# Attention into two expert stages: PSUM banks handed out a second time, sums of squares on other engines, copies queued behind the sigmoids

## The chip, the cores and the metric

One core of one Trainium2 chip. The metric is device microseconds of one launch. TensorE (PE) does the matrix products, with a queue of its own for weight loads (PEld); ScalarE (ACT), VectorE (DVE) and GpSimd (POOL) do the rest; SyncE's queue (SP) issues nearly all transfers. Each engine takes its instructions in the order in which the program gives them out. PSUM, in which products are accumulated, has eight banks of 512 f32 per partition.

## The reference

```python
# q, k, v: 4 x 12 heads x 448 x 64, f32
attn = 1 / (1 + exp(-(q @ k.T / 8 - log(448))))          # a sigmoid, no softmax
x = (attn @ v), heads side by side                       # 1792 x 768
xn = x / sqrt(mean(x * x) + 1e-6) * rms_g
g = xn @ w_gate;  val = xn @ w_val                       # 768 -> 1536
x = (g * sigmoid(g) * val) @ w_out                       # 1536 -> 768
logits = x @ gate                                        # 8 experts
out = top probability * (relu(x @ w1[e]) @ w2[e])        # the token's expert e
```

## The kernel before, in words

The order of all instructions is written out by hand; a helper adds the semaphores, from which instructions touch which tile.

**Attention** (L498, driven by the loop at L1054) takes 84 steps t, 21 (`QS`) for each of four batches. A step puts eight score products on PE (`quarters`, L528) into a PSUM tile of two banks, `two[t % 2]`; ACT takes the sigmoid (`weights`, L534) into SBUF; two steps later PE multiplies by v (`weighted`, L545) into two of the banks `one`. Seven steps do two pairs of heads. When a pair is done, `both` (L567) has ACT copy one bank (L575) and, a step later, DVE add the other (L576): that is x. `squares` (L579) then has POOL square x (L585, L582 for a batch's first pair) and add it to the batch's sum (L586). In step t, `step()` gives out what has come due, ahead of `weights(t)`; `then(1, ...)` called just before `step()` comes due in that same call.

`normalise` (L614) runs beside the next batch's steps: PE sums over partitions (L618), four small DVE operations, twelve on POOL (L633 to L636), ACT spreads the result (L640), PE turns it (L644), ACT copies it (L646), and DVE scales x in six steps (L650); batch 0 is also split in two for the exact products (ACT L670, DVE L675), the others go to DRAM. The last batch's `normalise` is a part of the attention generator and runs beside the first expert stage.

Beside attention, 64-bit weights are loaded and narrowed to 32 bits by three DVE operations each (`narrow`, L213, L217, L221; 36 pieces, 108 operations): one per call of `next(conv)` at L1068, the rest within the first batch of the first expert stage, where `operations_due` (L52) says how many. From the 13th piece on, the result goes to DRAM out of two buffers `wn` (L228).

**First expert stage** (`moe1`, L279, for each of four batches): 12 units of gate and value products, then 6 of the output product. A unit is four pieces of nine 128x128x448 products (`three`, L270, lines L273 to L275). A unit of the first kind has two banks, `pg` and `pv`, of `mm_bank`, three banks given out in turn. Two pieces after `pg` is started ACT takes its sigmoid (L281), DVE multiplies by `pg` (L282); after the next unit's first piece DVE multiplies by `pv` (L287), ACT and DVE split the result (L288, L289). An output unit has one bank; ACT copies it (L314), DVE subtracts and transposes it (L317, L320). Weights are split for the next unit by ACT (L243) and DVE (L246).

**Second expert stage** (L1184): four batches of 14 blocks, eight on w1 into `mm` banks (evicted by ACT L760 and DVE L761) and six on w2 into `sc` banks (DVE L781, L782); routing and the tokens of other experts run between blocks (L900, L924).

The banks of these two stages are slices of attention's tiles (L152 to L157):

```python
two = [ps.tile([128, 2, 512], F32, tag="two", name=f"two{i}", bufs=2) for i in range(2)]
one = [ps.tile([128, 512], F32, tag="one", name=f"one{i}", bufs=4) for i in range(4)]
fixed["mm"] = [two[0][:, 0, :], two[0][:, 1, :], two[1][:, 0, :]]
fixed["sc"] = [two[1][:, 1, :], one[3]]
fixed["av"] = [one[0], one[1]]
fixed["mi"] = [one[2]]
```

So two `mm` banks belong to the tile `two0`, and the third shares `two1` with an `sc` bank. `logit_bank` (L308) is the `mi` bank, and in the last batch one taken out of `mm`.

Of the kernel before, what the change touches and what calls it, by code (L numbers as in the profile page):

```python
# [9 lines left out]
F32 = mybir.dt.float32  # L10
# [38 lines left out]
LAG = 2  # L49


def operations_due(n):  # L52

    return int(n < 60 and n % 3 < 2)


CONST = {}
# [36 lines left out]
def block_kernel(ctx, tc, qkp, v, wg, wv, wo, g, gate, w1, w2, consts, out):  # L94
# [3 lines left out]
    def opened(name, side="left", **kw):  # L98
        s = ExitStack()
        return s, s.enter_context(tc.tile_pool(name=name, bufs=1, side=side, **kw))  # L100

    s_c, cpool = opened("cpool")
    s_d, dram = opened("dram", space=DRAM)
    s_p, ps = opened("ps", space=PSUM)
    s_k, keep = opened("keep")
    s_w, wp = opened("wp", reuse_waits="tile")
    s_x, xp = opened("xp", reuse_waits="tile")
# [43 lines left out]

    two = [ps.tile([128, 2, 512], F32, tag="two", name=f"two{i}", bufs=2) for i in range(2)]  # L152
    one = [ps.tile([128, 512], F32, tag="one", name=f"one{i}", bufs=4) for i in range(4)]
    fixed["mm"] = [two[0][:, 0, :], two[0][:, 1, :], two[1][:, 0, :]]
    fixed["sc"] = [two[1][:, 1, :], one[3]]
    fixed["av"] = [one[0], one[1]]
    fixed["mi"] = [one[2]]  # L157

    clock = [0]
    due = {}  # L160
# [337 lines left out]
    def attention():  # L498

        sums, score, weight = {}, {}, {}  # L500
        halves = [slice(0, D), slice(D, 2 * D)]
        last = NC - 1
        order = []
        for u in range(0, B * H // 2, 2):
            order += [(u, c) for c in range(NC)] + [(u + 1, c) for c in range(last)]
        due_at = {}
        now = [0]
        av = [one[0][:, :S], one[1][:, :S]]
        odd = [one[2][:, :S], one[3][:, :S]]

        def then(steps, f, *a):
            due_at.setdefault(now[0] + steps, []).append((f, a))

        def step():
            now[0] += 1
            for f, a in due_at.pop(now[0], []):
                f(*a)

        def quarters(t):
            u, c = order[t]  # L520
            for x, h in enumerate(halves):
                for i, o in enumerate(halves):
                    if c < last:
                        r, head, k = raw_a[u], h, S + 128 * c + D * i
                    else:

                        r, head, k = raw_a[u + x], halves[x ^ i], S + 128 * c
                    nc.tensor.matmul(  # L528
                        two[t % 2][o, x, :S], r[head, k : k + D], r[head, :S], start=True, stop=True
                    )  # L530

        def weights(t):
            a = aq.tile([128, 2, S], F32, tag="a", name="a", bufs=3)
            nc.scalar.activation(  # L534
                out=a, in_=two[t % 2][:, :, :S], func=AF.Sigmoid, bias=logs, scale=1.0 / math.sqrt(D)
            )
            weight[t] = a

        def add_up(u, c, x, i, a):

            v4 = raw_v[u].rearrange("s (c j d) -> s c j d", j=2, d=D)
            y = u % 2
            k = x ^ i ^ y
            first, end = (0, last if k == 0 else last - 1) if y == 0 else (last if k == 0 else 0, last - 1)
            nc.tensor.matmul(  # L545
                sums[u][k][halves[x]], v4[halves[i], c, x, :], a[halves[i]], start=(c == first), stop=(c == end)
            )

        def weighted(t):
            u, c = order[t]  # L550
            a = weight.pop(t)
            if c == 0 and u % 2 == 0:
                sums[u] = av
            elif c == 0:
                sums[u] = odd
            if c == last:
                sums[u + 1] = odd
            for x in range(2):
                for i in range(2):
                    if c < last:  # L560
                        add_up(u, c, x, i, a[:, x, :])
                    else:
                        add_up(u + x, c, x ^ i, i, a[:, x, :])
            if c == last - u % 2:
                then(1, both, u)

        def both(u):  # L567
            b, p = divmod(u, H // 2)
            if p == 0:
                pool, tag = (aq, "xt") if b % 2 else (keep, "x2_")  # L570
                xts[b] = [pool.tile([128, S], F32, tag=f"{tag}{k}", name="xt") for k in range(KD)]
                sss[b] = aq.tile([128, S], F32, tag="ss", name="ss", bufs=2)
            x = xts[b][p]
            p0, p1 = (sums[u][1], sums[u][0]) if u % 2 else (sums[u][0], sums[u][1])
            nc.scalar.copy(out=x, in_=p0)  # L575
            then(1, lambda: nc.vector.tensor_tensor(out=x, in0=p1, in1=x, op=ALU.add))  # L576
            then(2, squares, b, p)

        def squares(b, p):  # L579
            x = xts[b][p]  # L580
            if p == 0:
                nc.gpsimd.tensor_tensor(out=sss[b], in0=x, in1=x, op=ALU.mult)  # L582
            else:
                sq = aq.tile([128, S], F32, tag="sq", name="sq")
                nc.gpsimd.tensor_tensor(out=sq, in0=x, in1=x, op=ALU.mult)  # L585
                nc.gpsimd.tensor_tensor(out=sss[b], in0=sss[b], in1=sq, op=ALU.add)  # L586

        load_pair(0)
        load_v(0)
        load_pair(1)  # L590
        normal = iter(())
        for t in range(B * QS + LAG):
            if t < B * QS:
                u, c = order[t]
                if c == 0:
                    load_v(u + 1)
                    load_pair(u + 2)
                quarters(t)
            if t >= LAG:
                weighted(t - LAG)  # L600
            step()
            if t < B * QS:
                weights(t)
            if t >= QS and t % QS == 5:
                normal = normalise(t // QS - 1, odd[1])
            next(normal, None)
            yield
        while due_at:
            step()
            yield  # L610
        yield
        yield from normalise(B - 1, one[3])

    def normalise(b, bank):  # L614
        xt, ss = xts[b], sss[b]
# [16 lines left out]
        for _ in range(3):  # L632
            nc.gpsimd.tensor_tensor(out=ta, in0=ya, in1=ya, op=ALU.mult)  # L633
            nc.gpsimd.tensor_tensor(out=ta, in0=ta, in1=va, op=ALU.mult)
            nc.gpsimd.tensor_scalar(out=ta, in0=ta, scalar1=1.5, scalar2=None, op0=ALU.add)
            nc.gpsimd.tensor_tensor(out=ya, in0=ya, in1=ta, op=ALU.mult)  # L636
        yield
        yield
        yb = aq.tile([CT, NC, 128], F32, tag="yb", name="yb")
# [410 lines left out]
        yield  # L1050


    att = attention()
    for n in range(B * QS + LAG):  # L1054
        next(att)
        if n < RAW:
            load_64(n)
        if n == 10:
            nc.sync.dma_start(out=cst, in_=consts)
            nc.sync.dma_start(out=g_sb, in_=g)  # L1060
            nc.sync.dma_start(out=gate_sb, in_=gate)
        if n == 15:
            nc.scalar.copy(out=gate_2[:, :, :E], in_=gate_sb)
            nc.vector.tensor_tensor(
                out=gate_2[:, :, E:], in0=gate_sb, in1=f32(gate_2[:, :, :E]), op=ALU.subtract
            )
        if 2 <= n < 40 or n % 4 < 3:
            next(conv)  # L1068
        tick()
        if n in (60, 62):  # L1070
            split_w(0, n // 2 - 30)
    for b in range(B):
        routing = route(b - 1) if b > 0 else iter(())
        coming = iter(())
        for n, _ in enumerate(moe1(b)):
            next(att, None)
            if n == 4 * KF and b + 1 < B:
                coming = bring_x(b + 1)
            next(coming, None)
            tick()  # L1080
            if b == 0:
                if to_store:
                    c, w = to_store.pop(0)
                    nc.sync.dma_start(out=w32d[c // 2][c % 2], in_=w)
                for _ in range(operations_due(n)):
                    next(conv, None)
            elif n >= 2 and n % 2 == 0:
                next(routing, None)
            if b == 3:
                if n == 0:  # L1090
                    s_a.close()
                    s_r.close()
                    open_raw()
                    load_x(0)
                    e0 = own_expert(0)
                if n >= 2 and n % 2 == 0 and n < 2 * KD + 2:
                    load_row(w1, ph2["w1r"], e0, n // 2 - 1)
                if n == 49:
                    s_x.close()
                    ph2["s1"], ph2["ring1"] = opened("ring1", side="right", reuse_waits="tile")  # L1100
                if n in (62, 66):
                    split_block((n - 62) // 4)
        if b + 1 == B:
            settle()
# [160 lines left out]
```

## Time and profile before

| | us |
|---|---|
| median of three runs | 1023.4 (1023.02 to 1023.63) |
| the profiled execution, its own time | 1022.94 |
| its span, first to last instruction | 1021.2 |

The profile shows one execution. Its span is 1.74 us shorter than that execution's time. PE is busy for 93% of the span, DVE 53%, ACT 35%, POOL 9%; a busy PE is modelled with overlapping products, so intervals from start to start say more than durations. "Idle before" names what ended an engine's wait.

### The profile page before, as it was taken

The page shows a single profiled execution, that of the slowest core. Times are in us where ns is not written, and L with a number is a line of the kernel's source. Part 1 is how long each engine was busy: PE and PEld are TensorE (multiplying, and loading weights), DVE is VectorE, ACT ScalarE, POOL GpSimd, SP SyncE. Part 2 cuts the span into 40 slices and gives each one's busy share as a digit, 9 for nine tenths or more (in the row PEclk, how much of TensorE's full clock was granted, in tenths as well). Part 3 has the DMA queues.
Part 4 walks back from the last instruction along what each step waited for, and adds up shares of the span by engine and source line. Part 5 has one row for each costly group of instructions (what it writes and reads, how often), then busy time and mean ns, then how long its engine had stood idle before and what let it go on. Part 6 is the DMA issues. An engine that isn't in the chain of part 4 may idle for free.

```text
span 1021.2 us, 14782 instructions
## 1 busy us (share of the span) xinstructions
PE 953.7 (93%) x5646; PEld 782.7 (77%) x5646; DVE 546.2 (53%) x890; ACT 352.3 (35%) x508; POOL 87.5 (9%) x103
## 2 busy tenths in 40 slices
PE   8989998999999999999998999999988999989997
PEld 3434347888878888888887888889878878878887
DVE  5886777776435544435644436444355634334345
ACT  5676762323323333323333323332222132222130
POOL 1555553000000000000000000000000000000000
PEclk9999999999999999999999999999999999999999
DMA  8959988765753324562434694335376749829633
GB/s 322 335 198 350 327 315 281 272 235 184 222 167 94 109 93 147 171 180 75 124 102 148 173 317 175 122 93 143 113 210 241 202 146 334 283 69 318 167 55 57
DMA packets 128509, 195.72 MB, mean 192 GB/s; under 512 B 63321, under 2 KB 85209, under 8 KB 128432
## 3 DMA queue, kind: packets, MB, share of 16 engines
q1 hardware_dynamic: 120832, 192.58, 57.7%
q10 hardware_dynamic: 7456, 1.61, 0.8%
q8 instruction: 45, 0.74, 0.3%
q0 software_dynamic: 144, 0.53, 0.3%
q14 instruction: 32, 0.26, 0.1%
HBM read 152.54 MB, written 42.00 MB: 191 GB/s over the span
## 4 chain that ended last, share of the span: by engine, by line
PE 83%; DVE 7%; ACT 3%; DMA 2%; issue 2%; POOL 1%; SPq 1%; ACTq 0%; DVEq 0%; POOLq 0%
PE two L273 23%; PE two L275 21%; PE two L274 21%; PE two L528 4%; PE one L545 4%; PE one L273 2%; PE one L275 2%; PE one L274 2%; DVE sg L287 1%; ACT sg L281 1%; PE two L900 1%; DVE hl L761 1%; ACT a L534 1%; DMA w<-in_wg 1%; DMA w32d<-w32h 1%
## 5 line engine op out<-in xcount | busy, mean ns | idle before, releaser
L273 PE MATMUL two<-xh,wh 128*128 128x448 f32 x576 | 214.8, 373 | 21.0 <-DVE sg L287 13.0
L275 PE MATMUL two<-xh,wl 128*128 128x448 f32 x576 | 210.7, 366 | 0.0
L274 PE MATMUL two<-xl,wh 128*128 128x448 f32 x576 | 210.6, 366 | 0.0
L246 DVE TENSOR_TENSOR wl<-w,wh 128x768 fp32r<-128x768 f32 x132 | 124.8, 949 | 33.6 <-ACT wh L243 29.2
L273 PEld LDWEIGHTS two<-xh,wh 128*128 128x128 f32 x576 | 108.2, 188 | 41.9 <-DVE sg L287 18.5
L243 ACT CAST wh<-w 128x768 fp32r<-128x768 f32 x132 | 109.7, 831 | 47.2 <-PE two L274 33.0
L273 PE MATMUL two<-hs,wh 128*128 128x448 f32 x288 | 106.7, 371 | 11.7 <-DVE xr L320 8.0
L275 PEld LDWEIGHTS two<-xh,wl 128*128 128x128 f32 x576 | 108.2, 188 | 9.1
L274 PEld LDWEIGHTS two<-xl,wh 128*128 128x128 f32 x576 | 108.3, 188 | 8.3
L275 PE MATMUL two<-hs,wl 128*128 128x448 f32 x288 | 105.3, 366 | 0.0
L274 PE MATMUL two<-hs,wh 128*128 128x448 f32 x288 | 105.3, 366 | 0.0
L288 ACT CAST hs<-sg 128x448 fp32r<-128x448 f32 x48 | 27.2, 568 | 183.4 <-DVE sg L287 183.4
L534 ACT ACTIVATE a<-two,logs 128x896 f32<-128x896 f32 x84 | 83.1, 1010 | 19.1 <-PE two L528 19.1
L528 PE MATMUL two<-rqk 64*64 64x448 f32 x672 | 82.9, 552 | 6.1 <-DMA rqk<-in_qkp 3.8
L273 PE MATMUL two<-xd,w1h 128*128 128x448 f32 x192 | 72.2, 376 | 12.0 <-DVE hl L761 12.0
L545 PE MATMUL one<-a,rv 64*64 64x448 f32 x672 | 81.5, 537 | 0.9 <-DMA rv<-in_v 0.9
L282 DVE TENSOR_TENSOR sg<-two,sg 128x448 f32<-128x448 f32 x48 | 29.8, 622 | 83.8 <-PE two L275 76.1
L273 PEld LDWEIGHTS two<-hs,wh 128*128 128x128 f32 x288 | 54.1, 188 | 22.0 <-DVE xr L320 10.3
L274 PE MATMUL two<-xd,w1h 128*128 128x448 f32 x192 | 70.8, 369 | 0.0
L275 PE MATMUL two<-xd,w1l 128*128 128x448 f32 x192 | 70.8, 369 | 0.0
L317 DVE TENSOR_TENSOR x2s<-two,x2s 128x448 fp32r<-128x448 f32 x24 | 15.0, 625 | 85.7 <-ACT x2s L314 47.9
L528 PEld LDWEIGHTS two<-rqk 64*64 64x64 f32 x672 | 25.4, 134 | 46.1 <-issue 22.6
(185 smaller groups left out, 1303.0 us busy)
## 6 DMA issues: line engine op xcount, KB each, us to landing
w<-w32d SPq DMA_DIRECT2D x132, 384.0 KB, 3.6
w1r<-in_w SPq DMA_DIRECT2D x24, 512.0 KB, 6.3
w2r<-in_w SPq DMA_DIRECT2D x32, 384.0 KB, 6.7
x2s<-x2s SPq DMA_DIRECT2D x48, 224.0 KB, 2.0
xd<-x2s SPq DMA_DIRECT2D x8, 1344.0 KB, 9.7
rqk<-in_qkp SPq DMA_DIRECT2D x23, 448.0 KB, 6.4
w<-in_wg SPq DMA_DIRECT2D x12, 768.0 KB, 6.6
w<-in_wv SPq DMA_DIRECT2D x12, 768.0 KB, 6.4
```

The source lines that it names most:

```text
L243: nc.scalar.copy(out=h, in_=w3)
L246: nc.vector.tensor_tensor(out=l, in0=w3, in1=f32(h), op=ALU.subtract)
L273: nc.tensor.matmul(p, wh, xh, start=(n == 0), stop=False)
L274: nc.tensor.matmul(p, wh, xl, start=False, stop=False)
L275: nc.tensor.matmul(p, wl, xh, start=False, stop=last)
L281: nc.scalar.activation(out=t, in_=p, func=AF.Sigmoid)
L282: later(1, lambda: nc.vector.tensor_tensor(out=t, in0=p, in1=t, op=ALU.mult))
L288: nc.scalar.copy(out=hs[:, 0, :], in_=t)
L317: nc.vector.tensor_tensor(out=l, in0=p, in1=f32(h), op=ALU.subtract)
L528: nc.tensor.matmul(two[t % 2][o, x, :S], r[head, k : k + D], r[head, :S], start=True, stop=True)
L534: nc.scalar.activation(out=a, in_=two[t % 2][:, :, :S], func=AF.Sigmoid, bias=logs, scale=1.0 / math.sqrt(D))
L545: nc.tensor.matmul(sums[u][k][halves[x]], v4[halves[i], c, x, :], a[halves[i]], start=(c == first), stop=(c == end))
```

## The change

PSUM is closed after attention and opened again as eight tiles of one bank each: three `mm`, two `sc`, two `av`, one `mi`. Squares move from POOL to ACT, and their sums to DVE a step later. `step()` comes after `weights(t)`, so what is due in a step is queued behind that step's sigmoid. `normalise` waits one more step ahead of L640. The conversions have another pattern: from step 2 on one in each step, none in steps 11 to 17 of each 21 from the second batch's on, and in the first expert stage three for each four pieces (48 places) where there were two for each three (40). The attention loop now runs until attention has nothing due, and the last `normalise` starts from the loop over `moe1`, in a new `sc` bank.

```diff
 def operations_due(n):
-    return int(n < 60 and n % 3 < 2)
+    return int(n < 64 and n % 4 < 3)
...
-    s_p, ps = opened("ps", space=PSUM)
+    s_p, ps = opened("ps", space=PSUM, reuse_waits="tile")
...
-    fixed["mm"] = [two[0][:, 0, :], two[0][:, 1, :], two[1][:, 0, :]]
-    fixed["sc"] = [two[1][:, 1, :], one[3]]
-    fixed["av"] = [one[0], one[1]]
-    fixed["mi"] = [one[2]]
...
             if p == 0:
-                nc.gpsimd.tensor_tensor(out=sss[b], in0=x, in1=x, op=ALU.mult)
+                nc.scalar.square(out=sss[b], in_=x)
             else:
                 sq = aq.tile([128, S], F32, tag="sq", name="sq")
-                nc.gpsimd.tensor_tensor(out=sq, in0=x, in1=x, op=ALU.mult)
-                nc.gpsimd.tensor_tensor(out=sss[b], in0=sss[b], in1=sq, op=ALU.add)
+                nc.scalar.square(out=sq, in_=x)
+                then(1, lambda: nc.vector.tensor_tensor(out=sss[b], in0=sss[b], in1=sq, op=ALU.add))
...
                 weighted(t - LAG)
-            step()
             if t < B * QS:
                 weights(t)
+            step()
...
         while due_at:
             step()
             yield
-        yield
-        yield from normalise(B - 1, one[3])
...
             nc.gpsimd.tensor_tensor(out=ya, in0=ya, in1=ta, op=ALU.mult)
+        yield
         yield
         yield
...
-    att = attention()
-    for n in range(B * QS + LAG):
-        next(att)
+    for n, _ in enumerate(attention()):
...
-        if 2 <= n < 40 or n % 4 < 3:
+        if n >= 2 and not (n >= QS and 11 <= n % QS < 18):
             next(conv)
...
+    s_p.close()
+    s_p, ps = opened("banks", space=PSUM, reuse_waits="tile")
+    for tag, n in (("mm", 3), ("sc", 2), ("av", 2), ("mi", 1)):
+        fixed[tag] = [ps.tile([128, 512], F32, tag=tag, name=f"{tag}_{i}", bufs=n) for i in range(n)]
+    att = normalise(B - 1, fixed["sc"][0])
...
         for n, _ in enumerate(moe1(b)):
-            next(att, None)
+            if b > 0 or n >= 3:
+                next(att, None)
```

## Rows read from the trace of the kernel before

**Rows 1.** Busy time by stretch, core 0: us, then each engine, PEclk, DMA share, GB/s.

```profile
3.00:150.40 147.40, 140.13 (x1393) 57.47 (x1393) 109.68 (x137) 99.86 (x122) 72.43 (x78) 1.00 0.86 313
150.40:1014.80 864.40, 813.57 (x4258) 725.18 (x4254) 435.12 (x749) 250.96 (x384) 14.88 (x22) 1.00 0.55 173
768.00:771.00 3.00, 3.00 (x9) 2.69 (x9) 0.09 (x1) 0.00 (x0) 0.00 (x0) 0.50 0.59 167
```

**Rows 2.** Waits in both expert stages, 150 to 1021 us: total, times, longest.

```profile
PE two L273 <- DVE hl L761: 14.4, 11, 2.1
...
PE two L273 <- DVE sg L287: 13.0, 17, 1.2
...
PE two L273 <- ACT sg L281: 8.0, 15, 0.7
PE two L273 <- DVE xr L320: 8.0, 6, 1.3
...
PE two L273 <- ACT x2s L314: 3.7, 6, 0.6
...
PE two L359 <- DVE hl L761: 1.3, 1, 1.3
PE two L924 <- DVE hl L761: 1.3, 1, 1.3
```

**Rows 3.** Timeline around one sigmoid of the first expert stage.

```profile
330.97 0.55 ACT L281 ACTIVATE sg<-two 128x448 f32<-128x448 f32 x1 [3.57 <-PE two L275]
...
331.57 0.47 PE L273 MATMUL two<-xh,wh 128*128 128x448 f32 x1 [0.37 <-ACT sg L281]
```

**Rows 4.** Timeline of PE at the last batch's change from w1 to w2.

```profile
985.01 0.36 PE L275 MATMUL two<-xd,w1l 128*128 128x448 f32 x1
985.22 0.36 PE L273 MATMUL one<-hh,w2h 128*128 128x448 f32 x1
...
986.82 0.36 PE L275 MATMUL one<-hh,w2l 128*128 128x448 f32 x1
```

**Rows 5.** Timeline of PE around one wait for L287.

```profile
318.38 0.36 PE L275 MATMUL two<-xh,wl 128*128 128x448 f32 x1
319.46 0.47 PE L273 MATMUL two<-xh,wh 128*128 128x448 f32 x1 [0.72 <-DVE sg L287]
319.76 0.36 PE L274 MATMUL two<-xl,wh 128*128 128x448 f32 x1
```

**Rows 6.** Timeline of PE at two long waits of the second expert stage.

```profile
765.13 0.37 PE L275 MATMUL two<-xd,w1l 128*128 128x448 f32 x1
767.28 0.47 PE L273 MATMUL two<-xd,w1h 128*128 128x448 f32 x1 [1.79 <-DVE hl L761]
...
813.07 0.47 PE L273 MATMUL two<-xd,w1h 128*128 128x448 f32 x1 [2.13 <-DVE hl L761]
813.38 0.36 PE L274 MATMUL two<-xd,w1h 128*128 128x448 f32 x1
813.58 0.36 PE L275 MATMUL two<-xd,w1l 128*128 128x448 f32 x1
```

**Rows 7.** Timeline of PE: two halves of an undisturbed attention step.

```profile
59.70 0.93 PE L528 MATMUL two<-rqk 64*64 64x448 f32 x8
60.46 0.93 PE L545 MATMUL one<-a,rv 64*64 64x448 f32 x8
```

**Rows 8.** Groups in attention, 3 to 150.4 us: busy, mean ns, idle before.

```profile
L534 ACT ACTIVATE a<-two,logs 128x896 f32<-128x896 f32 x84 | 83.1, 1010 | 19.1 <-PE two L528 19.1
...
L576 DVE TENSOR_TENSOR xt<-one,xt 128x448 f32<-128x448 f32 x23 | 14.3, 620 | 6.8 <-ACT xt L575 6.7
L575 ACT COPY xt<-one 128x448 f32<-128x448 f32 x23 | 12.2, 532 | 23.7 <-PE one L545 23.7
...
L644 PE MATMUL one<-cst,yb 112*128 112x112 f32 x24 | 3.4, 286 | 3.3 <-ACT yb L640 3.3
```

**Rows 9.** Waits in attention, 3 to 150.4 us.

```profile
PEld two L528 <- ACT a L534: 16.9, 22, 1.7
```

**Rows 10.** Transfers out of the tile wn.

```profile
DMA to landing us min/median/max: 2.3/2.9/7.6
```

**Rows 11.** Groups of the whole span: ACT's only load of function tables.

```profile
L126 ACT ACT_TABLE_LOAD x1 | 1.3, 1283 | 0.8 <-PEq L1255 0.8
```

## The prediction

> **What bounds the kernel now.** I read the busy time by stretch first. In both stages after attention PE is busy for 813.6 of 864.4 us at full clock, DVE for half of it, ACT for under a third [rows 1]: PE sets the time, and what can be won is what it waits for. The waits view of that stretch is the main view. PE waits 57 times for ACT or DVE, 49.7 us in all (14.4 + 13.0 + 8.0 + 8.0 + 3.7 + 1.3 + 1.3) [rows 2], and all of these are waits to write a bank while another instruction reads. The reader should ask whether it is the same bank. By the code it is not. The three `mm` banks go round as (0, 1), (2, 0), (1, 2) for `pg` and `pv` of three units. Banks 0 and 1 are halves of one tile. In the first sort of unit the sigmoid reads bank 0 while PE wants to go on in bank 1; behind the second, L287 reads bank 0 while the third writes bank 1. That makes four of each in 12 units, 16 in four batches: the trace has 15 and 17. Output units 1 and 4 use bank 0 and are followed by bank 1: six waits each for L314 and L320 in three batches; in the last batch bank 0 holds the logits and the two others lie in different tiles. That is all 44; the 13 for L761 also fall where neighbours share a tile.
>
> Two more views speak for sharing as the cause. The sigmoid on bank 0 was itself held for 3.57 us by products, though its own bank had been complete for a piece; it started when PE stopped writing the neighbour, and PE went on when it had ended [rows 3]. And where a w1 block in `two1` is followed by a w2 block in a bank of `one`, PE goes on after 0.21 us, its usual pace (1.60 us for eight intervals), with the same L760 and L761 behind it [rows 4].
>
> In attention PE is busy for 140.1 of 147.4 us [rows 1]. Its weight loads wait 22 times for a sigmoid [rows 9], about once for each of the 24 pairs: the copy L575 stands ahead of a sigmoid on ACT, and itself waits for that step's second half on PE (23.7 us idle before it [rows 8]).
>
> **Banks of their own.** A wait costs more than its idle time: from 318.38 to 319.76 PE makes two intervals in 1.38 us that otherwise take 0.40, so 0.98 is lost where 0.72 is shown as idle [rows 5]. With 0.26 more for each of 57: 49.7 + 14.8 = 64.5 us. Some waits stand behind short products that hide a part, so I take **63**, with ends 49.7 and 64.5. [...]
>
> What is late next? A bank is written again three pieces later at the earliest, some 5.4 us; the eviction is two or three operations of about 0.6 us. DVE has 435 us to do in what would be some 800, ACT 251 [rows 1]. Closest is the first batch, where conversions run beside: attention takes 66 of the 108 instead of 73, so 42 instead of 35 fall here. Seven of under 1 us each are hidden by DVE's free time. I set 2.5 us against all new waits, with ends 0 and 18 (rival 1). The hand-over of PSUM costs nothing if it waits by tile, as the tile's last sigmoid has run before the last products of attention start; if it waited for the whole pool, the last copy and addition (0.53 + 0.62 [rows 8]) would come first, once, and are within those 2.5.
>
> **Attention.** Half a step is 0.76 us [rows 7], so 84 steps are 127.7. L644 is busy for 3.4 us [rows 8], and I count as much again for the sums ahead of it. Of 147.4 us, 0.8 lie ahead of the first product; 12 remain as waits, and bound what these edits can win; a loss is rival 3. For ACT's spread factors PE waits 3.3 us [rows 8] in three goes, with restarts 4.1; the added step gives POOL's chain 1.5 us more each time, and POOL no longer has squares: I count 3. Of the other 8, the waits for sigmoids are the larger part and transfers at the start the rest: with the copy behind the sigmoid, the next sigmoid is late by some 0.1 us where PE's two tiles let it be late by 1. I count 6. Together **9**, ends 0 and 12.
>
> What this adds: ACT gets a square per pair. No row shows one; the nearest is the copy of the same shape, 0.53, the other end DVE's addition, 0.62 [rows 8]; I take the copy's, the same engine. Seven steps then hold 7 x 1.01 + 4 x 0.53 = 9.2 us of ACT in 10.6 of PE. While batch 0 is scaled its six splits, priced as the copy, come on top: 12.4, for one group of steps; overlapping starts take back some of it, and 1 us is within the 2.5. DVE gets 20 sums of 0.62 (12.4 us) and loses seven conversions; at 109.7 of 147.4 [rows 1] it has room. In its queue an addition stands behind a conversion, and a conversion can wait for a store out of `wn`: at one conversion per step there are two steps, 3 us, between a store and the buffer's next use, against a landing of 2.9 at the median and 7.6 at most [rows 10]. The square is not wanted before a step later, so the median is hidden and the worst case is not (rival 1). On SP, loads for the next pairs stand behind these stores but are issued two pairs ahead. The last batch's L640 also comes a piece later: 1 us, where PE waits for it too, estimated from the same wait in attention.
>
> **Sum.** Against the profiled execution: 1022.94 - 63 - 1.5 - 9 - 1 + 2.5 = 950.9. Its time is 0.46 under the median of the runs, so **951** for the median. About 0.2%, 2 us, is what a measurement can tell from no change.
>
> **Rivals.**
> 1. *PE gets new waits* (0.13): DVE late in attention's second half and in the first batch, where conversions wait for stores and the transfer queues are at 0.86 of their time in attention [rows 1]. With 1 us lost in each of the first batch's 18 units: 951 + 18 = 969; I let this case reach from 960 to 985. Against it: DVE's share, and the three pieces above.
> 2. *The waits stay* (0.06): the helper orders by something other than the tile, so the change does not do what it seems to. Only attention's 9 and the 1 are won: 1013. Against it: the counts above and the 0.21 us.
> 3. *Squares make ACT change function tables* (0.06), the way to a slower kernel. Each square then brings two loads of 1.28 us [rows 11], 3.1 us with its own time, ahead of a sigmoid. PE can run on for 1 us, so it loses about 2 at each of 24 squares: 951 + 48 = 999. [...] It is slower than before from 72 / 24 = 3.0 us per square on; I give that half of this chance. Against it: L575's copies and L760's relu run among sigmoids, with one load in the whole span [rows 11].
>
> [...]
>
> **Numbers.** As summed: 0.75, between 944 (all ends good) and 960. The range 944 to 975 takes this in and about half of rival 1. Faster by over 0.2%: 0.75 + 0.13 + 0.06 + 0.03, less 0.01 for the unforeseen; within 0.2%: 0.01; slower: 0.03, from rival 3.
>
> **What would show it.** Right: in both expert stages no wait of PE for L281, L287, L314, L320 or L761; sigmoids starting when their own products end; PE's stretch some 800 us; attention ending near 141; squares of about 0.53 us on ACT, and one table load. Wrong: waits of L273 for weights (L243, L246) in the first batch; sigmoids behind squares that wait for DVE; a second ACT_TABLE_LOAD; a PEclk under 1 in attention.

## The result, and the profile after

The changed kernel takes **948.33 us** (median of 4 runs, 948.02 to 949.03) against 1023.51 (4 runs, 1023.02 to 1023.81) beside it on the same chip: a ratio of 0.9267 with a 95% interval of 0.9251 to 0.9283. The profiled execution took 948.02 with a span of 946.1; line numbers from here on are those of the changed kernel, some four to six lower than before in the functions spoken of (the gate sigmoid is L277, was L281).

Busy time by stretch, attention and then both expert stages, in the columns of [rows 1]:

```profile
3.00:140.90 137.90, 135.63 (x1392) 55.65 (x1392) 90.28 (x143) 111.32 (x145) 16.37 (x36) 1.00 0.83 297
140.90:939.70 798.80, 797.62 (x4258) 727.33 (x4254) 449.03 (x763) 252.42 (x385) 12.37 (x19) 1.00 0.61 193
```

From the first product of the expert stages to the last, PE takes 798.7 us where it took 864.1: 65.4 less. Attention ends at 140.91 where it ended at 150.40: 9.5 less. The two make 74.9, which is the whole difference of the profiled executions (1022.94 - 948.02 = 74.92); the ends of the kernel did not move.

Waits from 136 us to the end of the changed kernel (engine, line, waited for: total, times, longest), the answer to [rows 2]. The first two rows are what the gate's sigmoid and the multiplication by `pv` (L283, was L287) wait for; the last two are all that PE has:

```profile
ACT sg L277 <- PE mm L271: 71.2, 45, 2.9
...
DVE sg L283 <- PE mm L271: 55.4, 39, 2.3
...
PE sc L639 <- ACT yb L635: 1.0, 1, 1.0
PE mi L423 <- DVE acc L419: 0.2, 1, 0.2
```

All 57 waits for an eviction are gone; PE waits twice in 800 us. The evicting engines wait for PE as they did before, only oftener: the sigmoid 45 times where it was 36, L283 39 times where L287 did 27 times. One sigmoid of the first expert stage, with PE around it, is the answer to [rows 3]:

```profile
288.89 0.37 PE L271 MATMUL mm<-xh,wl 128*128 128x448 f32 x1
...
289.10 0.37 PE L269 MATMUL mm<-xh,wh 128*128 128x448 f32 x1
...
289.30 0.55 ACT L277 ACTIVATE sg<-mm 128x448 f32<-128x448 f32 x1 [1.34 <-PE mm L271]
289.31 0.37 PE L270 MATMUL mm<-xl,wh 128*128 128x448 f32 x1
...
289.51 0.37 PE L271 MATMUL mm<-xh,wl 128*128 128x448 f32 x1
```

The product of 288.89 ends at 289.26 and the sigmoid starts at 289.30. PE goes on at its pace of 0.20 to 0.21 us through the whole sigmoid, which takes the same 0.55 us as before: here writing one bank while ACT reads the next costs neither anything.

In attention, the waits from 3 to 142 us that answer to [rows 9] and to the spread factors of [rows 8]:

```profile
PEld two L524 <- ACT a L530: 2.7, 6, 1.1
PE one L639 <- ACT yb L635: 1.5, 2, 0.9
DVE wn L209 <- DMA w32d<-wn: 1.0, 1, 1.0
```

Weight loads waited 22 times for a sigmoid, 16.9 us; now 6 times, 2.7. The waits for the spread factors fell from 3.3 us to 1.5 and did not go. The groups of the same engines, over the whole span (the first row) and from 3 to 140 us (the others):

```profile
L126 ACT ACT_TABLE_LOAD x1 | 1.3, 1283 | 0.8 <-PEq L1254 0.8
```
```profile
L571 ACT COPY xt<-one 128x448 f32<-128x448 f32 x23 | 12.1, 525 | 0.0
...
L582 DVE TENSOR_TENSOR ss<-ss,sq 128x448 f32<-128x448 f32 x18 | 11.3, 625 | 18.8 <-ACT sq L581 18.8
L581 ACT ACTIVATE sq<-xt 128x448 f32<-128x448 f32 x19 | 10.8, 567 | 0.0
```

A square takes 0.567 us, ACT never loads another function table, and the copy (L571) no longer stands 23.7 us idle ahead of a queue of sigmoids [rows 8].

### The profile page after: what moved, and what is told of

Read it like the earlier page. It is cut to its first block, busy times and chain, and to the rows that moved or that the text cites. A ratio compares the mean times of both kernels' runs of the same rounds, so it can differ in the third digit from the quotient of the medians.

```text
span 946.1 us, 14817 instructions
## 1 busy us (share of the span) xinstructions
PE 933.4 (99%) x5646; PEld 783.0 (83%) x5646; DVE 540.7 (57%) x910; ACT 365.2 (39%) x532; POOL 28.9 (3%) x59
## 4 chain that ended last, share of the span: by engine, by line
PE 96%; POOL 2%; ACT 1%; DVE 0%; issue 0%; DMA 0%; POOLq 0%; SPq 0%; DVEq 0%; ACTq 0%
PE mm L269 22%; PE mm L270 22%; PE mm L271 22%; PE two L524 6%; PE one L541 6%; PE sc L269 4%; PE sc L270 4%; PE sc L271 4%; PE sc L919 1%; PE mm L895 1%; PE mi L355 1%; POOL ta L627 1%; POOL ta L629 1%; POOL ya L630 0%; PE one L639 0%
## 5 line engine op out<-in xcount | busy, mean ns | idle before, releaser
L269 PE MATMUL mm<-xh,wh 128*128 128x448 f32 x576 | 211.7, 367 | 0.0
L270 PE MATMUL mm<-xl,wh 128*128 128x448 f32 x576 | 210.6, 366 | 0.0
L271 PE MATMUL mm<-xh,wl 128*128 128x448 f32 x576 | 210.6, 366 | 0.0
L269 PEld LDWEIGHTS mm<-xh,wh 128*128 128x128 f32 x576 | 108.2, 188 | 9.9 <-issue 0.7
L271 PEld LDWEIGHTS mm<-xh,wl 128*128 128x128 f32 x576 | 108.2, 188 | 8.9
L270 PEld LDWEIGHTS mm<-xl,wh 128*128 128x128 f32 x576 | 108.2, 188 | 8.7
L269 PE MATMUL mm<-hs,wh 128*128 128x448 f32 x288 | 105.5, 366 | 0.0
L270 PE MATMUL mm<-hs,wh 128*128 128x448 f32 x288 | 105.4, 366 | 0.0
L271 PE MATMUL mm<-hs,wl 128*128 128x448 f32 x288 | 105.3, 366 | 0.0
L530 ACT ACTIVATE a<-two,logs 128x896 f32<-128x896 f32 x84 | 84.6, 1008 | 24.0 <-PE two L524 22.5
L269 PE MATMUL mm<-xd,w1h 128*128 128x448 f32 x192 | 70.9, 369 | 0.0
L270 PE MATMUL mm<-xd,w1h 128*128 128x448 f32 x192 | 70.2, 366 | 0.0
L271 PE MATMUL mm<-xd,w1l 128*128 128x448 f32 x192 | 70.2, 365 | 0.0
L283 DVE TENSOR_TENSOR sg<-mm,sg 128x448 f32<-128x448 f32 x48 | 29.9, 624 | 55.4 <-PE mm L271 55.4
```

What stands on the lines that cost most here:

```text
L269: nc.tensor.matmul(p, wh, xh, start=(n == 0), stop=False)
L270: nc.tensor.matmul(p, wh, xl, start=False, stop=False)
L271: nc.tensor.matmul(p, wl, xh, start=False, stop=last)
L283: nc.vector.tensor_tensor(out=t, in0=p, in1=t, op=ALU.mult)
L530: nc.scalar.activation(out=a, in_=two[t % 2][:, :, :S], func=AF.Sigmoid, bias=logs, scale=1.0 / math.sqrt(D))
```

## The experiments

My theory: the banks are worth 65 us because waits go by tile, and the rest of the change is worth 9 to 10 in attention. The rival to the first half: the gain comes from another order of work, or from fewer than all the shared tiles. For the second half I had no rival of one piece; so each part was undone by itself. All changes are made to the changed kernel unless it says otherwise; times are medians of 4 runs. "Stage" is again PE's stretch from the first to the last product of the expert stages.

**1. The banks alone.** The kernel before with the new banks, the loop that runs on, and the last normalisation moved into the expert stage; squares, order, conversions and the steps of `normalise` as before:

```diff
-                nc.scalar.square(out=sss[b], in_=x)
+                nc.gpsimd.tensor_tensor(out=sss[b], in0=x, in1=x, op=ALU.mult)
...
             if t < B * QS:
+                step()
                 weights(t)
-            step()
...
```

> The kernel before with the eight one-bank tiles alone (and what they need: the attention loop runs until nothing is due, and the last normalise starts from the first expert stage's loop). Theory (PE's waits come from banks sharing a tile): the 57 waits go and nothing else, 1023.5 - 65 = 958 to 960, attention still ending near 150. Rival (the expert stages gain from POOL or DVE being relieved): only part of the 65, above 975.

Measured: 960.21 (958.08 to 961.15), ratio 0.9385 (0.9367 to 0.9404), a fifth of a microsecond above what was expected. The stage takes 798.96, 65.1 less than before, and attention ends at 150.45, where it ended before. In the stage the waits view has two rows for PE:

```profile
PE sc L638 <- ACT yb L634: 1.6, 1, 1.6
PE mi L423 <- DVE acc L419: 0.2, 1, 0.2
```

So all of the stage's gain, but for 0.3 us, belongs to the banks.

**2. Everything but the banks.** The change on the old slices of attention's tiles:

```diff
-    s_p.close()
-    s_p, ps = opened("banks", space=PSUM, reuse_waits="tile")
...
+    fixed["mm"] = [two[0][:, 0, :], two[0][:, 1, :], two[1][:, 0, :]]
+    fixed["sc"] = [two[1][:, 1, :], one[3]]
...
```

> The changed kernel with the banks as slices of attention's tiles, as before. Theory: all 57 waits are back, 948.3 + 65 = 1013 to 1015, and attention still ends near 141. Rival (the parts need one another): attention's end moves too, or the sum of this gain and that of the banks alone misses 75 us by more than 2.

Measured: 1010.36 (1010.13 to 1011.16), ratio 0.9874 (0.9854 to 0.9893). Attention ends at 140.55, as early as with the banks; the stage takes 861.5, 2.6 less than before, which I had not expected. Two things make up most of it. L283 is waited for 15 times and 11.3 us, and L278 once for 0.8, where L287 was 17 times and 13.0; the conversions fall elsewhere in that stage, which may be why, and was not tried. And the clock does not fall. The kernel before has a fall worth 1.5 us behind its wait of 1.79 us ([rows 6, 1]); here the same two long waits, 1.79 and 2.13 us, leave it at full speed:

```profile
800.42 0.47 PE L269 MATMUL two<-xd,w1h 128*128 128x448 f32 x1 [2.13 <-DVE hl L756]
```
```profile
800.00:803.00 3.00, 2.58 (x13) 2.40 (x14) 1.24 (x2) 0.00 (x0) 0.00 (x0) 1.00 1.04 237
```

Against the kernel before as it ran beside them (1023.6) the halves gain 63.4 and 13.2 us, 76.6 in sum, where the whole change gains 75.2: they are independent within 1.4, and the fall of the clock that experiment 2 was spared is as large as that.

**3. One tile of two banks.** Two of the three `mm` banks are made halves of one tile again. They are the same banks of PSUM, and no instruction moves:

```diff
-    for tag, n in (("mm", 3), ("sc", 2), ("av", 2), ("mi", 1)):
+    pair = ps.tile([128, 2, 512], F32, tag="pair", name="pair", bufs=1)
+    for tag, n in (("mm", 1), ("sc", 2), ("av", 2), ("mi", 1)):
...
+    fixed["mm"] = [pair[:, 0, :], pair[:, 1, :]] + fixed["mm"]
```

> The changed kernel, PSUM opened anew, but two of the three mm banks are halves of one tile of two banks; each bank lies at the same address as in the changed kernel. Theory (the tile, not the bank, is what is waited for): the 44 waits for the gate, value and output evictions come back and some 10 of the 13 for the relu's, 54 waits of about 1.1 us: 1004 to 1010. Rival (opening the pool anew, or its reuse by tile, is what counted): 948, no wait.

Measured: 1008.14 (1007.64 to 1008.41), ratio 0.985 (0.9831 to 0.9869). PE's waits from 136 us on:

```profile
PE pair L269 <- DVE sg L283: 11.2, 15, 0.9
PE pair L269 <- DVE hl L756: 10.7, 8, 2.1
PE pair L269 <- DVE xr L316: 8.0, 6, 1.3
PE pair L269 <- ACT sg L277: 8.0, 15, 0.7
PE pair L269 <- ACT x2s L310: 3.7, 6, 0.6
```

These five rows hold 50 waits and 41.6 us, nearly those of [rows 2]; with three single ones, 3.4 us, they are 53. The stage is 60.1 us longer. **This settles the cause**: same banks, same order, same operations, and only the tile that two of the banks belong to differs between 948 and 1008 us.

**4. The same with the two `sc` banks**, a pair that was not shared before:

```diff
-    for tag, n in (("mm", 3), ("sc", 2), ("av", 2), ("mi", 1)):
+    for tag, n in (("mm", 3), ("av", 2), ("mi", 1)):
...
+    fixed["sc"] = [pair[:, 0, :], pair[:, 1, :]]
```

> The changed kernel with the two sc banks as halves of one tile; in the kernel before they lay in different tiles, so no wait for them was seen in any trace. Theory: PE then waits at each w2 block that follows another, for the transpose of its neighbour (0.65 us and about 0.3 around it): some 20 waits of about 1 us in the second expert stage, 948.3 + 20 = 964 to 972, none in the first. Rival (only mm banks matter, for some other reason): 948.

Measured: 967.96 (967.46 to 969.41), ratio 0.9462 (0.9442 to 0.9481). The waits are new ones, where the theory puts them:

```profile
PE pair L269 <- DVE yt L776: 13.5, 17, 0.8
PE pair L269 <- DVE ys L925: 1.1, 2, 0.6
...
PE pair L919 <- DVE yt L776: 0.7, 1, 0.7
```

They also test the price of a wait. The prediction added 0.26 us for the restart to each wait's idle time: 15.3 + 20 x 0.26 = 20.5. The stage grew from 798.7 to 818.8, by 20.1. In experiment 3 the sum is 45.0 + 53 x 0.26 = 58.8, against 60.1. The rest there is the clock, which falls behind the second of the two long waits, where it fell behind the first in the kernel before. Ten products then take 3.6 us instead of 2.05, so 1.5 is lost:

```profile
799.35 0.48 PE L269 MATMUL pair<-xd,w1h 128*128 128x448 f32 x1 [2.13 <-DVE hl L756]
```
```profile
800.00:803.00 3.00, 3.00 (x10) 2.65 (x9) 0.16 (x1) 0.00 (x0) 0.00 (x0) 0.50 1.03 201
```

**5. Copies ahead of the sigmoids again**:

```diff
             if t < B * QS:
+                step()
                 weights(t)
-            step()
```

> The changed kernel with what is due in a step (copies and squares on ACT) given out ahead of that step's sigmoid again. Theory (the order is the largest part of attention's 9.5 us): PE's weight loads wait for sigmoids some 22 times again, attention ends 5 to 9 us later than 140.9, 953 to 957. Rival (relieving POOL and DVE made the gain, not the order): within 1.5 us of 948.3.

Measured: 954.4 (953.47 to 954.78), ratio 0.9319 (0.9303 to 0.9334), as the theory has it. Attention ends 4.9 us later, a little short of its 5 to 9. The stage is 1.4 us longer without a new wait of PE; that is a slower pace of the same products, shown under experiment 7. Waits from 3 to 147 us:

```profile
PEld two L524 <- ACT a L530: 21.0, 28, 1.1
```

The 22 waits of [rows 9] are back, and six more; the square that now stands in the same queue is the likely reason.

**6. Squares and their sums on GpSimd** (`nc.gpsimd.tensor_tensor` for the two `nc.scalar.square` and the addition, as in the kernel before):

> The changed kernel with squares and their sums on POOL again. Theory: POOL's squares keep VectorE's two-operand conversions longer and POOL's short chain later, but VectorE has room and the spread of the factors has a step more: 948.3 + 0 to 3. Rival (contention between POOL and VectorE was what held attention): 4 us or more.

Measured: 951.93, ratio 0.929 (0.9264 to 0.9315); the four times are 949.6, 949.9, 954.0 and 954.1. The median lies between the theory, at most 951.3, and the rival, at least 952.3. The profiled execution is one of the longer: attention is 1.4 us longer, the stage 4.8. There the last normalisation comes late, and the clock falls behind it to 0.50. PE, and two stretches of busy time with the granted clock as the third number from the end:

```profile
162.09 2.05 PE L639 MATMUL sc<-cst,yb 112*128 112x112 f32 x8 [2.13 <-ACT yb L635]
163.82 0.72 PE L269 MATMUL mm<-xh,wh 128*128 128x448 f32 x1
```
```profile
160.00:162.00 2.00, 0.00 (x0) 0.00 (x0) 0.46 (x1) 0.58 (x1) 1.13 (x4) 0.99 1.05 349
162.00:164.00 2.00, 1.92 (x9) 1.92 (x10) 0.00 (x0) 0.03 (x1) 0.00 (x0) 0.50 0.96 355
```

**7. The same with that wait covered**, by one `yield` more in the last batch's normalisation. A `yield` in `normalise` is one whole step of attention, some 1.5 us (84 steps in 127.7 us), or one piece of the expert stage, some 1.85 us; the expectations here and in experiment 11 call it a half step:

```diff
         yield
+        if b == B - 1:
+            yield
         yb = aq.tile([CT, NC, 128], F32, tag="yb", name="yb")
```

> The kernel with the squares back on GpSimd (951.93 us, 3.6 above the changed kernel), with one half step more in the last batch's normalisation alone, where that kernel showed a wait of 2.1 to 2.3 us and behind it 3 us at a granted clock of 0.50. Theory: the cost of the squares on GpSimd was that one wait and the clock behind it, not the squares as such: the wait and the half-clock stretch go, 948.5 to 950 us, all runs within 1 us of each other. Rival: squares on GpSimd slow VectorE's work beside them and cost that for themselves: 952 us or more, attention's ending 1.5 us or more later than in the changed kernel.

Measured: 948.76 (948.25 to 950.42), ratio 0.9255 (0.9234 to 0.9276). The wait is down to 0.3 us and the clock does not fall in attention or in the stage. The median is as the theory has it; that all runs lie within 1 us of each other is not, they spread over 2.2. In the profiled execution, the longest of the four, attention still ends 1.0 us later than in the changed kernel, so about that much there belongs to the squares; by the medians it is 0.4 in all. The stage is 3.7 us shorter than in experiment 6, which is the wait and the clock.

The stage is still 1.1 us longer than in the changed kernel, though PE waits less there. The same products run at a slower pace. From 170 to 230 us, this kernel and then the changed one:

```profile
170.00:230.00 60.00, 60.00 (x292) 54.54 (x291) 50.65 (x71) 21.14 (x34) 0.00 (x0) 1.00 0.83 290
```
```profile
170.00:230.00 60.00, 60.00 (x298) 55.62 (x297) 51.27 (x71) 22.13 (x35) 0.00 (x0) 1.00 0.83 288
```

At the same clock and with PE busy throughout, 292 products run where 298 did. The gate's sigmoids, which start when their own products end, follow each other every 7.44 us for most of the first batch (192.75, 200.19, 207.63), and every 7.30 in the changed kernel (191.81, 199.11, 206.41). The profiled executions of experiments 5 and 6 show 7.44 too, that of experiment 11 shows 7.30. What sets the pace is open; it is worth some 1.5 us, so a difference of that size between two executions need not come from an edit.

**8. The old pattern of the conversions**:

```diff
-    return int(n < 64 and n % 4 < 3)
+    return int(n < 60 and n % 3 < 2)
...
-        if n >= 2 and not (n >= QS and 11 <= n % QS < 18):
+        if 2 <= n < 40 or n % 4 < 3:
```

> The changed kernel with the conversions in the pattern of before (73 or more of 108 beside attention, also while x is scaled). Theory: in batch 0's scaling VectorE is behind and a sigmoid or two wait, 948.3 + 0.5 to 2.5; the expert stages do not move. Rival (more conversions beside the first batch are a cost that this takes away): 946 to 948.

Measured: 956.03 (954.44 to 957.19), ratio 0.9333 (0.9315 to 0.9352): 7.7 us more, **a miss**, where I had 2.5 at most. Attention ends 6.1 us later, and the stage, which was not to move, is 2.8 longer. The longest stop in attention, on PE, on DVE, and in a stretch of busy time behind it:

```profile
81.47 0.93 PE L541 MATMUL one<-a,rv 64*64 64x448 f32 x4
83.88 0.97 PE L541 MATMUL one<-a,rv 64*64 64x448 f32 x4 [1.48 <-DVE wn L209]
```
```profile
83.22 0.56 DVE L209 TENSOR_SCALAR wn<-w 128x768 int32<-128x768 int32 x1 [2.11 <-DMA w32d<-wn]
```
```profile
86.00:88.00 2.00, 2.00 (x16) 0.66 (x12) 1.83 (x6) 0.52 (x1) 1.21 (x3) 0.50 1.02 415
```

DVE stood for 2.1 us at a conversion whose buffer `wn` was still being stored, PE went on only when that conversion had run, and then its clock was granted at 0.50. Which of DVE's results PE was really held for isn't in the records. In the stage a wait of 1.9 us for the spread factors, from 164 us on, is followed by the same fall of the clock, to 0.50 from 168 to 170 us.

**9. The pause kept for batch 0 alone**:

```diff
-        if n >= 2 and not (n >= QS and 11 <= n % QS < 18):
+        if n >= 2 and not QS + 11 <= n < QS + 18:
```

> The pause of the conversions is kept only while batch 0 is scaled and dropped while the others are. Without any pause the kernel took 956.03 us, 7.7 more than the changed kernel. Theory: what the pause saves lies in batch 0's scaling, where ScalarE and VectorE also split x (sigmoid waits of 0.6 to 0.9 us) and where the store that follows came late (a stop of 2.0 us at 81 us, then half clock): 948 to 950.5 us. Rival: the loss without the pause lies in the later batches (a wait of 1.9 us for the spread factors at 164 us with half clock behind it), and this kernel shows them again: 952 to 956 us.

Measured: 951.38 (951.07 to 951.48), ratio 0.9282 (0.9262 to 0.9303), between the two theories: of the 7.7 us of experiment 8 this kernel has 4.7 back, and 3.0 are still missing. Experiment 8 also had three conversions in four steps from step 40 on, and the older places in the expert stage, so the 4.7 are the pause in batch 0 together with these; the 3.0 are the later pauses alone. Their mechanism is neither theory's. Waits from 3 to 142 us, and busy time from 90 to 142, of this kernel and then of the changed one:

```profile
DVE wn L209 <- DMA w32d<-wn: 8.1, 7, 1.9
...
PE one L541 <- DMA rv<-in_v: 1.2, 2, 0.7
```
```profile
90.00:142.00 52.00, 50.84 (x520) 21.52 (x521) 41.15 (x64) 41.36 (x54) 4.71 (x12) 1.00 1.02 374
```
```profile
90.00:142.00 52.00, 51.14 (x533) 21.80 (x526) 34.49 (x55) 41.90 (x55) 6.03 (x12) 1.00 0.83 299
```

Conversions that run on bring their loads and stores forward with them. From 90 us on the transfer queues are at 1.02 of their time instead of 0.83, and PE waits for v twice, which it does not in the changed kernel; by its start times the two stops lose 1.9 of the 2.5 us by which attention ends later. So the pause also thins out the transfers.

**10. Without the added step**: the `yield` ahead of L635 that the change added is taken out.

> The changed kernel without the added step ahead of the spread of the factors. Theory: PE waits 1.5 us at most longer for it in each of three batches and once in the first expert stage: 950 to 954. Rival (POOL's chain is shorter now that POOL has no squares, so the step is not needed): 948 to 949.

Measured: 954.15 (951.16 to 954.76), ratio 0.9321 (0.9305 to 0.9336), 0.15 above the theory's upper end. Waits from 3 to 250 us:

```profile
PE one L638 <- ACT yb L634: 4.3, 3, 2.2
...
PE sc L638 <- ACT yb L634: 1.7, 1, 1.7
```

The profiled execution is the shortest of the four, 3.1 above that of the changed kernel: 2.3 in attention and 0.6 in the stage. What the other three have on top was not seen.

**11. One step more** in each of the four normalisations, in three of which PE still waits in the changed kernel:

```diff
         yield
+        yield
         yb = aq.tile([CT, NC, 128], F32, tag="yb", name="yb")
...
-        if n >= 2 and not (n >= QS and 11 <= n % QS < 18):
+        if n >= 2 and not (n >= QS and 12 <= n % QS < 19):
```

> One more half step between the inverse root and the spreading of it, in all three normalisations; the pause of the conversions is moved by one half step with it. In the changed kernel TensorE still waits for the spread factors once in each normalisation: 0.86, 1.04 and 1.15 us, 3.05 us in all. Theory: those waits are the only ones left in attention and its end, and a half step (3 to 4 us) covers each. Expected 945 to 947 us, TensorE's waits for yb gone from the list. Rival: the scaling moves by a half step too and runs into the next heads, so that the weighted sums then wait for the factor instead; expected 948 to 951 us, with new waits for the copies of the head pairs.

Measured: **945.29** (944.53 to 945.74), ratio 0.9224 (0.9204 to 0.9245), below both kernels. PE's whole list of waits, from 3 to 142 us and then from 136 on, is

```profile
PE two L524 <- DMA rqk<-in_qkp: 3.8, 1, 3.8
...
PE mi L423 <- DVE acc L419: 0.2, 1, 0.2
```

The waits for the factors are gone and the time is 3.0 us shorter. The expectation read these waits too high: by the rows of the changed kernel they are 0.68, 0.86 and 0.98 us, the 1.5 and 1.0 shown above, 2.5 in all. With 0.26 for each restart that is 3.3. One step of 1.5 us covers each; the 3 to 4 us that the expectation gives a half step are not what it lasts.

**12. GpSimd's twelve small products on VectorE** (`nc.vector` for `nc.gpsimd` in L627 to L630):

> The twelve small products of the inverse root go from GpSimd to VectorE, nothing else. In the changed kernel the chain that ends in the wait for the spread factors runs through GpSimd, twelve operations one behind the other. Theory: on VectorE the twelve are shorter, the chain ends earlier and the three waits (0.86, 1.04, 1.15 us) go: 945 to 947 us. Rival: VectorE takes them in turn behind conversions of about 1 us each, so the chain ends later than now: waits for yb of 2 us or more, 949 to 955 us.

Measured: 945.5 (944.91 to 946.15), ratio 0.9223 (0.9202 to 0.9244). One line of the chain in both kernels, in the groups from 3 to 170 us, this one first:

```profile
L627 DVE TENSOR_TENSOR ta<-ya 112x4 f32<-112x4 f32 x12 | 1.9, 160 | 0.3
```
```profile
L627 POOL TENSOR_TENSOR ta<-ya 112x4 f32<-112x4 f32 x12 | 9.0, 753 | 131.1 <-DVE va L624 130.5
```

The waits for the factors are gone, and only one new wait of 0.6 us came (for `sg`, L278, at 151 us). The two remedies gain the same, so behind these waits stood the chain's length against the steps given to it.

## Why the prediction was right

It said 951 us, with 944 to 975 as its range, and gave 0.75 to the case that came.

**Own banks**: 63 us and 1.5 for the clock, 64.5; measured 65.4 in the stage, 65.1 with the banks alone. The reading that carried it was that PE's waits named an eviction of *another* bank, with counts that fit the neighbours in one tile; experiments 3 and 4 show it by making such pairs anew. The surcharge of 0.26 us for each wait holds at both. The 1.5 for the clock is half of the 3 us at 0.50 behind the wait of 1.79 us in the kernel before ([rows 6, 1]). It is of the right size, but that it was there to be won is luck: with the same two waits the clock fell once in experiment 3 and not at all in experiment 2.

**Attention**: 9 us; measured 9.5. Its two parts are of the right size when each is undone alone: the order of the copies 4.9 against 6, the added step 2.3 against 3. But the new pattern of the conversions, for which it set no gain, is worth 6.1 in attention, and the squares 1.0 to 1.4. These do not add: undone singly they cost 4.9 + 2.3 + 6.1 + 1.4 = 14.7 of a gain of 9.5. The lists of waits in experiments 5 to 10 suggest why: each covers the same few waits, and one that is uncovered can cost the clock as well, as in experiments 6 and 8 (0.50 behind it). So the mechanism named for the two parts was right, but that the sum of a list without its largest item came within 0.5 us is in part luck.

**Last normalisation**: 1 us; measured none. PE waits 1.0 us for it before and after. It waits 1.7 without the added step (experiment 10) and 1.6 with the banks alone (experiment 1), so the new start cost some 0.7 and the step gave that back.

**Allowance for new waits**: 2.5 us, the term that was missed most. Nothing of it was spent, and the forecast without it is 948.4, against 948.02 profiled; that this is so near is luck too, as the banks and attention gave 1.4 us more than forecast and the last normalisation 1 less. The prediction set it against conversions in the first batch of the expert stage and against the worst landing of a store [rows 10]. DVE waited for such a store once in attention, 1.0 us, and PE did not wait behind it. Experiment 8 shows what the allowance was for, in the pattern that the change gave up.

**Rival 1** (new waits of PE) fell with the waits view. **Rival 2** (the waits stay) fell with experiment 1, and experiment 3 shows how it would have looked: 1008, near its 1013. **Rival 3** (squares force table loads): there is one load in the span, of 1.28 us, as before, with 24 squares among the sigmoids: here the square ran beside the sigmoid without a further load. A square was priced at the copy's 0.53 and took 0.567.

Right as named: no wait of PE for L277, L283, L310, L316 or L756; a stretch of 798.7 for "some 800"; attention's end at 140.9 for "near 141"; PEclk at 1.00 in both stretches.

## What to carry to other kernels

Where PE waits for an eviction, ask which bank it writes and which is being read; if they differ, look for one tile around both, and give each bank a tile of its own. Price such a wait at its idle time and a restart, here 0.26 us. When a bound engine has few waits left, undo each protection alone before calling it worthless: what seems to cost nothing may be holding the same wait closed as its neighbour.

## What the hardware showed that I had not expected

**DVE's conversions are faster without the squares on GpSimd.** The prediction gave the move of the squares off GpSimd no such effect. The same conversion, from 3 to 140 us, with the squares on GpSimd (experiment 6) and then in the changed kernel:

```profile
L213 DVE SCALAR_TENSOR_TENSOR w32h<-w,w32h 128x768 int32<-128x768 int32 x12 | 16.0, 1330 | 0.2
...
L209 DVE TENSOR_SCALAR w32h<-w 128x768 int32<-128x768 int32 x12 | 9.8, 815 | 10.7 <-DMA w<-in_wg 10.7
```
```profile
L213 DVE SCALAR_TENSOR_TENSOR w32h<-w,w32h 128x768 int32<-128x768 int32 x12 | 11.4, 953 | 0.2
...
L209 DVE TENSOR_SCALAR w32h<-w 128x768 int32<-128x768 int32 x12 | 6.6, 554 | 10.1 <-DMA w<-in_wg 10.1
```

That is 0.38 and 0.26 us for each operation. The expectation of experiment 6 named the two-operand conversions: L213 reads two tensors, but L209 reads one and is longer too. The addition L572, which reads a PSUM bank and a tile of SBUF, takes 0.62 us in both kernels. What parts the slower operations from this one is open.

**The clock falls after some waits of about 2 us and not after others.** It was granted at 0.50 behind idle times of 1.79 (before, [rows 6]), 2.1 (experiment 6) and 1.5 to 1.9 us as the waits show them (experiment 8, twice); it stayed at 1 behind 2.13 [rows 6] and 2.2 (experiment 10). In the second expert stage the same two waits, 1.79 and 2.13 us, come in three kernels: the clock fell behind the first in the kernel before, behind the second in experiment 3, and behind neither in experiment 2. So the length of the wait alone does not decide, and what does is open. The four times of experiment 6 lie in two pairs 4 us apart, and the one that was profiled, of the longer pair, has such a fall and the slower pace of experiment 7; that the shorter ones lack them was not seen.
